# Gated recurrence and multiplicative feed-forward on one core: another layout for the first 512 tokens, ten operations for the decay rates, a last tile in two strips, and another order of the first fifteen chunks

## The chip, the core and the metric

The kernel runs on one core of a Trainium2 chip. A core has a matrix engine (TensorE, in the profile PE, its weight loads PEld), a vector engine (VectorE, DVE), a scalar engine (ScalarE, ACT), GpSimd (POOL) and SyncE (SP), which here issues the transfers. Each engine runs its own instructions strictly in the program's order and waits on semaphores for the others. The metric is the device time of one execution in microseconds; lower is better.

## The reference

The first half is a gated linear recurrence over 4 sequences of 5,824 tokens with 256 channels, the second a feed-forward block on the 23,296 tokens, with a product of two projections in its middle:

```python
# x, r_gate, i_gate: (4, 5824, 256); a_param: (256,)
a_base = 1.0 / (1.0 + np.exp(-a_param))
sig_r = 1.0 / (1.0 + np.exp(-r_gate));  sig_i = 1.0 / (1.0 + np.exp(-i_gate))
log_a = 8.0 * sig_r * np.log(np.clip(a_base, 1e-06, 1.0 - 1e-06))[None, None, :]
a_t = np.exp(log_a)
norm = np.sqrt(np.maximum(1.0 - a_t * a_t, 1e-06))
x_gated = norm * sig_i * x
for t in range(S):
    h = a_t[:, t] * h + x_gated[:, t]
    y[:, t] = h
# y as 23296 x 256; w1, w2: 256 x 1024; w3: 1024 x 1024; w_out: 1024 x 256
h = (y @ w1) * (y @ w2) @ w3
out = (h @ w_out).astype(np.float32)
```

## The kernel before

The 23,296 tokens are cut into 47 chunks, `sizes = [256, 256] + [512] * 44 + [256]`. Gates of chunks 0 and 1 are made together, as one of 512 tokens (`gates_of`, `width`, `part`). The kernel is a list of small steps, written out by hand as one string, `ORDER`; each word names a step and its chunk, and each engine gets its instructions in the order of the words. So a word further left on one engine can hold up everything behind it on that engine, and the transfers, all issued by SP, go in the order of their words too.

The words, for chunk c:

- `r i x`: loads of the three inputs (512 KB each); `Lw1. Lw2. Lw3. Lwo.` loads of weight pieces (512 KB each), `Cw1.` and so on their casts to bf16 on the engine that `W_ACT`, `W_DVE` or, failing both, GpSimd gives (L385, L387).
- `R I`: tanh of r and of i on ACT (L157, L159, L165). `p t`: plus one, times x (L170, L186, L189). `V U`: turning channels to partitions, on PE against the identity through PSUM (L197) or by a transposing transfer (L208), for r and for the gated x.
- `d`: the decay by an exponential (L220). `s`: its square (L228, L230; `DV_SQUARE` and `AC_SQUARE` give the engine). `q`: the root (L235). `g`: root times gated x on DVE (L245, L248). `h`: the scan on DVE (L266), one for each half of the channels. `y`: cast of the scan's result to bf16 (L278).
- `a c.m.q`: one up product with w1, two matmuls into one PSUM bank (L289, tile pa). `b c.m`: two up products with w2 (tile pb). `c c.m.q`: copy of pa to SBUF as bf16 (tile sa; L303 on DVE, L305 on ACT, by `DV_COPY`). `m c.m`: the product of sa and pb on DVE (L317, tile g_t).
- `D c.j`: the down product of 128 tokens, eight matmuls of 256 columns (L331, tile po) with a matrix folded from w3 and w_out. `e o`: its copy to SBUF and the store.
- `Ft Fc Fm Fe`: the folding itself, transpose of a piece of w3 (L392), copy, product with w_out (L403), copy (L438, L440).
- `A3. A0. A1. A2.`: the decay rates of the 256 channels from `a_param` (L412 to L434). `E`: the identity in bf16. `W`: two matmuls of the identity whose result nobody reads (L283, tile warm).

The tiles are rings of fixed size, among them `"r": 4, "i": 5, "x": 4`, and in PSUM `"po": 4` banks, which pa, po and all the turned tiles share, and `"pb": 2` of two banks each. A step that takes a slot waits for the reader of what was in it: with two pb slots, a `b` waits for the `m` two `b`s earlier; with four po slots, an `a` waits for the copy of the tile four earlier.

For chunks 0 and 1 every pa tile holds 256 columns of a bank of 512, and has its own copy of 128x256. In the last chunk (46) each `D` has its own PSUM tile, `e` alternates between DVE and ACT, and each 128 tokens are stored by one transfer.

Of the kernel before, what the change touches and what calls it, by code (L numbers as in the profile page):

```python
# [18 lines left out]
LOG1P = (2.00000001, 0.66666316, 0.40024854, 0.27961419, 0.28174657)  # L19
# [3 lines left out]
def kernel(  # L23
# [71 lines left out]
    DV_EVAC = {(2, 0), (8, 0), (8, 1), (9, 0), (9, 1)}
    FOLD_ACT = {('c', 7), ('e', 3), ('e', 4)}
    W_ACT = {('w1', 1), ('w2', 0), ('w3', 0)}
    W_DVE = set()
# [3 lines left out]
    WARM = [2] * 16  # L102
    RINGS = {"r": 4, "i": 5, "x": 4, "th_r": 3, "u": 2, "rt": 2, "ut": 6, "a": 6, "nrm": 6, "h": 2, "y": 4,
# [38 lines left out]
    def load(c, nm):  # L142
        n = width(c) // P
        t = ring(loads, [P, 4, D], F32, name=nm + "_t", tag=nm)
        nc.sync.dma_start(
            out=t[:, :n, :],
            in_=src[nm][starts[c]:starts[c] + width(c), :].rearrange("(p n) c -> p n c" if long_rows(c) else "(n p) c -> p n c", p=P))
        T[nm, c] = t
# [102 lines left out]
    def scan(c, cb):  # L251
        w = sizes[c]
        first = ("h", c) not in T
        if first:
            T["h", c] = ring(ypool, [P, NCB, CT], F32, name="h_t", tag="h")
        h = T["h", c][:, :, :w]
        a, n = (T[key, gates_of(c)][:, :, part(c)] for key in "an")
        if first:
            for b in range(1, B):
                if 0 < b * S - starts[c] < w:  # L260
                    nc.vector.memset(a[:, :, b * S - starts[c]:b * S - starts[c] + 1], 0.0)
        init = 0.0
        if starts[c] % S != 0:
            pw = sizes[c - 1]
            init = T["h", c - 1][:, cb, pw - 1:pw]
        nc.vector.tensor_tensor_scan(h[:, cb, :], a[:, cb, :], n[:, cb, :], init, ALU.mult, ALU.add)  # L266

    def cast(c, cb=None):
        w = sizes[c]
        if ("y", c) not in T:  # L270
            T["y", c] = ring(ypool, [P, NCB, CT], BF16, name="y_t", tag="y")
        key = c if cb is None else (c, cb)
        cbs = slice(None) if cb is None else cb
        y, h = T["y", c][:, cbs, :w], T["h", c][:, cbs, :w]
        if key in AC_CAST:
            nc.scalar.copy(out=y, in_=h)
        else:
            (nc.vector if key in DV_CAST else nc.gpsimd).tensor_copy(out=y, in_=h)  # L278

# [6 lines left out]
    def up(c, m, dst, w_sb):  # L286
        w = sizes[c]
        for cb in range(NCB):
            nc.tensor.matmul(out=dst[:, :w], lhsT=w_sb[:, cb, m * P:(m + 1) * P],  # L289
                             rhs=T["y", c][:, cb, :w], start=(cb == 0), stop=(cb == NCB - 1))  # L290

    def up_a(c, mp, q):
        T["pa", c, mp, q] = pp = ring(psum_o, [P, CT], F32, name="pa", tag="po")
        up(c, 2 * mp + q, pp, w1_sb)

    def up_b(c, mp):
        T["pb", c, mp] = pp = ring(psum_b, [P, 2, CT], F32, name="pb", tag="pb")
        for q in range(2):
            up(c, 2 * mp + q, pp[:, q, :], w2_sb)
# [7 lines left out]
    def copy(c, mp, q):  # L307
        w = sizes[c]
        if ("sa", c, mp) not in T:
            T["sa", c, mp] = ring(ffn, [P, 2, CT], BF16, name="sa", tag="sa")  # L310
        copy_to((c, mp, q) in DV_COPY, T["sa", c, mp][:, q, :w], T["pa", c, mp, q][:, :w])

    def product(c, mp):
        w = sizes[c]
        if ("g", c) not in T:
            T["g", c] = ring(ffn, [P, KD, CT], BF16, name="g_t", tag="g")
        nc.vector.tensor_mul(out=T["g", c][:, 2 * mp:2 * mp + 2, :w], in0=T["sa", c, mp][:, :, :w],  # L317
                             in1=T["pb", c, mp][:, :, :w])

    def pair(c, j2):  # L320
        return min(2, sizes[c] // P - 2 * j2)

    def down(c, j):
        if c == NCH - 1:
            T["po_last", j] = po = ring(psum_o, [P, D], F32, name="po", tag="po")
        else:
            if ("po", c, j // 2) not in T:
                T["po", c, j // 2] = ring(psum_o, [P, 2, D], F32, name="po", tag="po")
            po = T["po", c, j // 2][:, j % 2, :]
        for k in range(KD):  # L330
            nc.tensor.matmul(out=po,  # L331
                             lhsT=T["g", c][:, k, j * P:(j + 1) * P], rhs=wp_sb[:, k, :],
                             start=(k == 0), stop=(k == KD - 1), skip_group_check=True)
# [6 lines left out]
    def evac_last(c, j):  # L340
        if ("ot", c, j // 2) not in T:
            T["ot", c, j // 2] = ring(ffn, [P, 2, D], F32, name="ot", tag="ot")
        copy_to(j % 2 == 0, T["ot", c, j // 2][:, j % 2, :], T["po_last", j])

    def store_last(c, j):
        t0 = starts[c] + j * P
        nc.sync.dma_start(out=out[t0:t0 + P, :], in_=T["ot", c, j // 2][:, j % 2, :])
# [41 lines left out]
    def fold_t(mi):  # L389
        pt = ring(psum_o, [P, KD, P], BF16, name="ptw", tag="po")  # L390
# [25 lines left out]
    def rates_abs():  # L416
        nc.vector.tensor_copy(out=la4, in_=T["la"])
        nc.vector.scalar_tensor_tensor(out=zz, in0=la4, scalar=-1.0, in1=la4, op0=ALU.mult, op1=ALU.min)
# [5 lines left out]
    def rates():  # L424
        nc.vector.tensor_scalar(zd, zz, 2.0, None, op0=ALU.add)
        nc.vector.reciprocal(zd, zd)
        nc.vector.tensor_mul(out=zz, in0=zz, in1=zd)
# [14 lines left out]
    def last(c):  # L442
# [3 lines left out]
        "r": lambda c: load(c, "r"), "i": lambda c: load(c, "i"), "x": lambda c: load(c, "x"),  # L446
# [17 lines left out]
        r0 i0 x0 A3. E A0. A1. A2. R0.1 R0.0 W7 W10 V0.1 V0.0 W3 W14 W4 d0.1 s0.1 d0.0 s0.0 I0 q0.0 t0.0 t0.1 U0 g0  # L464
        h0.0 W1 W2 W12 W5 W13 W8 W0 W15 h0.1 q0.1 g1 h1.1 h1.0 Lw1.0 Cw1.0 y0.1 y0.0 i2 Lw2.0 I2 r2 Lw1.1 Cw2.0 a0.0.1
        a0.0.0 a0.1.0 a0.1.1 b0.0 R2 Cw1.1 x2 y1.1 y1.0 p2 t2.0 Lw3.2 Cw3.2 Lw2.1 Lwo.1 t2.1 c0.0.1 c0.1.1 c0.0.0
        c0.1.0 m0.0 V2 b0.1 a1.1.0 a1.1.1 b1.1 a1.0.1 d2.1 d2.0 s2.1 s2.0 q2 m0.1 c1.1.1 c1.1.0 m1.1 c1.0.1 a1.3.0
        b1.0 a1.0.0 a0.2.0 c0.2.0 c1.0.0 c1.3.0 Cw2.1 Ft2 W9 Fc2 a0.2.1 a1.3.1 U2 a1.2.0 m1.0 W11 b0.2 c0.2.1 c1.3.1
        c1.2.0 Cwo.1 Lwo.0 Cwo.0 g2 r3 r4 Lw3.1 i3 Lw3.0 Lw3.4 Lw3.5 x3 Lw3.3 Lw3.7 Lw3.6 i4 m0.2 h2.0 h2.1 R3 a0.3.1
        W6 a0.3.0 b0.3 c0.3.0 c0.3.1 a1.2.1 Fm2 b1.2 V3 R4 c1.2.1 V4 d3.0 d4.1 d3.1 d4.0 m0.3 y2 b1.3 Fe2 m1.2 m1.3  # L470
        a2.1.0 a2.0.1 b2.0 Cw3.1 a2.0.0 Ft1 I3 c2.0.0 c2.0.1 c2.1.0 Fc1 a2.2.0 b2.1 Fm1 m2.0 c2.2.0 Cw3.0 s4.0 p3
        Cw3.4 s3.1 s4.1 s3.0 q3 q4 Ft0 a2.1.1 Fe1 Fc0 c2.1.1 Cw3.5 t3.0 t3.1 Ft4 a2.3.1 Fc4 c2.3.1 Fm0 Ft5 Fm4 a2.2.1
        Fe4 c2.2.1 Cw3.7 Cw3.3 Cw3.6 Fe0 Fc5 m2.1 U3 g3 Fm5 a2.3.0 Ft7 b2.3 Ft3 c2.3.0 Fe5 h3.1 h3.0 r7 I4 Fc7 R7 Ft6
        b2.2 Fm7 V7 r5 R5 Fc3 Fm3 Fc6 Fe7 d7.1 Fe3 y3 a3.1.1 d7.0 s7.0 c3.1.1 x4 i5 r6 Fm6 i6 i8 I5 R6 V5 p4 t4.0 t4.1
        x5 r8 m2.3 Fe6 m2.2 b3.1 a3.1.0 a3.2.1 a3.2.0 c3.1.0 c3.2.1 I6 V6 U4 b3.2 a3.0.1 D0.1 D0.0 g4 h4.0 h4.1 c3.0.1
        c3.2.0 d5.1 I8 e0.0 d5.0 s7.1 a3.0.0 m3.1 c3.0.0 D1.1 a3.3.1 D1.0 a3.3.0 R8 c3.3.1 e1.0 d6.0 p5 y4 t5.0 t5.1
        s5.1 p6 m3.2 c3.3.0 r10 x6 r9 i7 o1.0 o0.0 r12 x8 V8 a4.1.0 b3.3 m3.3 b3.0 a4.1.1 c4.1.0 s5.0 d6.1 s6.0 s6.1
        a4.2.0 b4.1 a4.0.1 a4.0.0 m3.0 c4.1.1 c4.0.1 c4.0.0 q7 q5 D3.0 D3.1 q6 c4.2.0 m4.1 a4.3.1 U5 g5 h5.0 h5.1
        c4.3.1 e3.0 R9 I7 b4.0 D2.3 D2.1 a4.2.1 D2.0 D2.2 c4.2.1 e2.1 m4.0 e2.0 b4.2 p8 t6.1 t6.0 y5 R10 t8.0 p7 t8.1
        a4.3.0 U6 a5.0.0 a5.1.0 b4.3 d8.1 c4.3.0 c5.0.0 d8.0 R12 s8.0 i10 m4.2 g6 h6.1 h6.0 x7 o3.0 r11 y6 D3.3 a5.0.1  # L480
        a5.1.1 c5.0.1 D3.2 c5.1.0 e3.1 I10 b5.1 m4.3 a5.2.1 a5.2.0 b5.0 V9 c5.1.1 m5.1 i9 V10 o2.0 o2.1 r16 i11 c5.2.1
        d9.1 I9 c5.2.0 d9.0 d10.0 R11 U8 i13 r13 x9 x10 V11 r15 m5.0 a6.0.1 a6.0.0 c6.0.1 c6.0.0 a6.1.1 b5.2 m5.2
# [151 lines left out]
```

## Time and profile before

| what | us |
|---|---|
| time, median of 3 runs (511.63 to 512.12) | 511.82 |
| the profiled execution's own time | 511.82 |
| its span in the profile | 510.0 |
| PE, ACT, DVE, POOL busy in the span | 502.2, 463.3, 429.8, 318.2 |
| first matmul of an up product starts | 13.30 |
| last matmul ends, about | 506.8 |

The span runs from the first instruction to the last; 1.8 us of the execution lie around it. Busy time is the union of an engine's instructions. In the views by time the first number is the start and the second a duration, both in microseconds; in the groups the numbers after the bar are the sum in microseconds and the mean of one in nanoseconds, and what stands in brackets or after the last bar is idle time before an instruction and who ended it.

### The profile page before, as it was taken

Reading aid. Unit: us, or ns where it says so; the run is one execution under the profiler, and the core shown is the slowest. Engines: PE = TensorE matmul, PEld = TensorE weight load, DVE = VectorE, ACT = ScalarE, POOL = GpSimd, SP = SyncE. Lnnn points to the kernel's source line nnn. Section 1 sums busy time; section 2 is a strip of 40 time slices with the busy share of each in tenths; the row PEclk is TensorE's granted clock in tenths of the full one; section 3 lists DMA queues with packets and bytes.
Section 4 is the critical chain, followed back from the end, with each engine's and each line's share of the span. In section 5 each row is a group of like instructions: output and inputs, shape, how many; then the busy total and the mean of one; then the engine's idle time right before and its main releaser. Section 6 shows DMA issues by size and latency. Waiting matters only on the chain.

```text
span 510.0 us, 8879 instructions
## 1 busy us (share of the span) xinstructions
PE 502.2 (98%) x3217; PEld 308.2 (60%) x3217; DVE 429.8 (84%) x417; ACT 463.3 (91%) x711; POOL 318.2 (62%) x274
## 2 busy tenths in 40 slices
PE   7999999999999999999999999999999999999997
PEld 3777655665565656556666556565566655656566
DVE  5999999999999789878879799878877797959762
ACT  7999999998999999999999999998998979888543
POOL 3775878557558936965786973956647568580200
PEclk9999999999999999999999999999999999999999
DMA  8999999999989997896999996898786895252313
GB/s 319 407 413 307 379 275 276 304 302 257 309 232 282 303 282 248 191 322 184 256 306 317 262 285 163 233 245 227 206 250 151 231 319 149 91 164 64 66 48 105
DMA packets 177904, 124.06 MB, mean 243 GB/s; under 512 B 87362, under 2 KB 173892, under 8 KB 177860
## 3 DMA queue, kind: packets, MB, share of 16 engines
q1 hardware_dynamic: 177856, 123.50, 85.2%
q8 instruction: 25, 0.41, 0.3%
q14 instruction: 19, 0.16, 0.1%
q10 hardware_dynamic: 4, 0.00, 0.0%
HBM read 78.91 MB, written 23.86 MB: 201 GB/s over the span
## 4 chain that ended last, share of the span: by engine, by line
PE 90%; ACT 4%; DVE 2%; issue 2%; DMA 1%; DVEq 0%; ACTq 0%
PE po L331 30%; PE pb L289 29%; PE pa L289 28%; PE pw L403 1%; ACT sa L305 1%; PE ptr L197 1%; DVE g_t L317 1%; DMA r_t<-in_r_gate_dram 1%; PE ptw L392 1%; DVE sa L303 1%; DVE h_t L266 1%; ACT L165 1%; ACT L235 1%; ACT nrm L235 0%; ACT i_t L165 0%
## 5 line engine op out<-in xcount | busy, mean ns | idle before, releaser
L317 DVE TENSOR_TENSOR g_t<-sa,pb 128x1024 bf16<-128x1024 bf16 (+1 forms) x188 | 218.6, 1180 | 60.6 <-PE pb L289 29.0
L289 PEld LDWEIGHTS <-w_sb 128*128 128x128 bf16 x1504 | 146.5, 98 | 144.0 <-issue 3.4
L305 ACT CAST sa<-pa 128x512 bf16<-128x512 f32 (+1 forms) x336 | 180.9, 588 | 27.7 <-PE pa L289 17.6
L289 PE MATMUL pa<-y_t,w_sb 128*128 128x512 bf16 (+1 forms) x752 | 190.6, 372 | 0.4 <-ACT sa L305 0.2
L289 PE MATMUL pb<-y_t,w_sb 128*128 128x512 bf16 (+1 forms) x752 | 185.2, 372 | 0.6 <-DVE g_t L317 0.6
L331 PE MATMUL po<-wp_sb,g_t 128*128 128x256 bf16 x1456 | 178.0, 273 | 0.0
L331 PEld LDWEIGHTS <-g_t 128*128 128x128 bf16 x1456 | 142.4, 98 | 40.6 <-issue 0.5
L278 POOL CAST y_t<-h_t 128x1024 bf16<-128x1024 f32 (+2 forms) x49 | 52.5, 1074 | 146.0 <-DVE h_t L266 142.2
L189 POOL TENSOR_TENSOR u_t<-i_t,x_t 128x512 bf16<-128x512 f32 (+1 forms) x90 | 122.2, 1374 | 4.1 <-issue 2.0
L266 DVE TENSOR_TENSOR_SCAN h_t<-a_t,h_t,nrm 128x512 f32<-128x512 f32 (+1 forms) x92 | 120.8, 1343 | 1.6
L230 POOL TENSOR_TENSOR nrm<-a_t 128x512 f32<-128x512 f32 x74 | 83.0, 1139 | 12.9 <-ACT a_t L220 10.1
L220 ACT ACTIVATE a_t<-rt,la 128x512 f32<-128x512 bf16 (+1 forms) x82 | 66.0, 823 | 0.0
L305 ACT COPY ot<-po 128x512 f32<-128x512 f32 x86 | 50.5, 591 | 12.0 <-PE po L331 11.8
L248 DVE SCALAR_TENSOR_TENSOR nrm<-nrm,ut 128x1024 f32<-128x1024 f32 (+1 forms) x39 | 53.3, 1368 | 5.8 <-ACT nrm L235 5.8
L170 POOL TENSOR_SCALAR i_t<-i_t 128x1024 f32<-128x1024 f32 (+1 forms) x44 | 52.9, 1204 | 7.9 <-ACT i_t L165 7.9
L165 ACT ACTIVATE i_t<-i_t 128x1024 f32<-128x1024 f32 (+1 forms) x46 | 48.9, 1064 | 0.1
L235 ACT ACTIVATE nrm<-nrm 128x1024 f32<-128x1024 f32 (+1 forms) x47 | 48.3, 1041 | 0.2
L159 ACT ACTIVATE th_r<-r_t 128x1024 bf16<-128x1024 f32 (+1 forms) x41 | 43.5, 1060 | 0.0
L303 DVE CAST sa<-pa 128x512 bf16<-128x512 f32 (+1 forms) x40 | 23.4, 615 | 0.6 <-PE pa L289 0.5
L235 ACT ACT_TABLE_LOAD x17 | 21.8, 1283 | 0.3
L165 ACT ACT_TABLE_LOAD x9 | 11.5, 1283 | 0.2
L283 PE MATMUL warm<-ident 128*128 128x512 bf16 x32 | 10.1, 457 | 0.0
(55 smaller groups left out, 119.3 us busy)
## 6 DMA issues: line engine op xcount, KB each, us to landing
r_t<-in_r_gate_dram SPq DMA_DIRECT2D x45, 512.0 KB, 5.3
i_t<-in_i_gate_dram SPq DMA_DIRECT2D x45, 512.0 KB, 5.6
x_t<-in_x_dram SPq DMA_DIRECT2D x45, 512.0 KB, 5.5
out_dram<-ot SPq DMA_DIRECT2D x90, 256.0 KB, 3.3
wf<-in_moe_w_dram SPq DMA_DIRECT2D x12, 512.0 KB, 10.5
wf<-in_moe_w_out_dram SPq DMA_DIRECT2D x2, 512.0 KB, 10.6
rt<-th_r SPq DMA_TRANSPOSE x41, 4.4
ut<-u_t SPq DMA_TRANSPOSE x39, 4.1
```

Source lines behind the costliest of these rows:

```text
L165: nc.scalar.activation(out=t[:, :n, :], in_=t[:, :n, :], func=AF.Tanh, scale=0.5)
L170: (nc.vector if c in DV_PLUS else nc.gpsimd).tensor_scalar(t, t, 1.0, 1.0, op0=ALU.add, op1=ALU.mult)
L189: (nc.vector if (c, half) in DV_HALF else nc.gpsimd).tensor_mul(out=u, in0=t, in1=xt)
L220: nc.scalar.activation(out=a, in_=pr, func=AF.Exp, scale=la4[:, cb:cb + 1], bias=la4[:, cb:cb + 1])
L230: (nc.vector if (c, cb) in DV_SQUARE else nc.gpsimd).tensor_mul(out=n, in0=a, in1=a)
L235: nc.scalar.activation(out=n, in_=n, func=AF.Sqrt, scale=-1.0, bias=1.0)
L248: nc.vector.scalar_tensor_tensor(out=n, in0=n, scalar=1e-3, in1=T["pu", c][:, :, cols], op0=ALU.max, op1=ALU.mult)
L266: nc.vector.tensor_tensor_scan(h[:, cb, :], a[:, cb, :], n[:, cb, :], init, ALU.mult, ALU.add)
L289: nc.tensor.matmul(out=dst[:, :w], lhsT=w_sb[:, cb, m * P:(m + 1) * P], rhs=T["y", c][:, cb, :w], start=(cb == 0), stop=(cb == NCB - 1))
L305: nc.scalar.copy(out=dst, in_=src_ps)
L317: nc.vector.tensor_mul(out=T["g", c][:, 2 * mp:2 * mp + 2, :w], in0=T["sa", c, mp][:, :, :w], in1=T["pb", c, mp][:, :, :w])
L331: nc.tensor.matmul(out=po, lhsT=T["g", c][:, k, j * P:(j + 1) * P], rhs=wp_sb[:, k, :], start=(k == 0), stop=(k == KD - 1), skip_group_che ...
```

## The change

- Chunks 0 and 1 share one h, one y and one g tile of 512 tokens. Their up products stay in halves of 256 tokens (`HALVED = 4` means all four pairs), but the two products q = 0 and 1 of a pair go into one PSUM bank and are copied together: 8 copies of 128x512 where there were 16 of 128x256. The down products of these 512 tokens are `D0.0` to `D0.3`, with two copies and two stores of 256 tokens.
- r of chunk 0 is one load (the `load` function gets an argument for half the columns, which no word uses).
- The rates: with z = exp(|x|), one over z + 0.5 takes the place of z / (z + 2), and the powers of two go into the constants: ten DVE operations in `A2.` where there were eleven.
- The last 128 tokens are two strips of 128 output columns: sixteen matmuls of 128 columns in two PSUM tiles, two copies (DVE, then ACT), two stores of 64 KB.
- `ORDER` is new from the start to chunk 14's scan; the 1,678 words behind that are the same. Which engine does which square, copy and cast is new up to chunk 15. The number of `W` words stays 16.

```diff
-LOG1P = (2.00000001, 0.66666316, 0.40024854, 0.27961419, 0.28174657)
+LOG1P = tuple(c / 2 ** (2 * k + 1) for k, c in
+              enumerate((2.00000001, 0.66666316, 0.40024854, 0.27961419, 0.28174657)))
...
-    DV_PLUS = {16}
+    DV_PLUS = set()
-    DV_SQUARE = {(0, 1), (11, 0)}
+    DV_SQUARE = {(0, 0), (0, 1), (5, 1), (9, 0)}
-    DV_CAST = set()
-    AC_CAST = set()
+    DV_CAST = {(1, 1)}
+    AC_CAST = {(1, 0)}
...
-    DV_EVAC = {(2, 0), (8, 0), (8, 1), (9, 0), (9, 1)}
-    FOLD_ACT = {('c', 7), ('e', 3), ('e', 4)}
-    W_ACT = {('w1', 1), ('w2', 0), ('w3', 0)}
-    W_DVE = set()
+    DV_EVAC = {(0, 0), (0, 1), (4, 1), (5, 1), (6, 1), (9, 0), (9, 1)}
+    FOLD_ACT = {('e', 0), ('e', 4), ('e', 5), ('e', 7)}
+    W_ACT = {('w2', 0), ('w3', 3)}
+    W_DVE = {('w1', 1)}
+    HALVED = 4
...
+    def in_half(c, mp):
+        return c < 2 and mp < HALVED
+
+    def span(c, mp):
+        return part(c) if in_half(c, mp) else slice(0, width(c))
...
     def up_a(c, mp, q):
+        if in_half(c, mp):
+            if ("pa", c, mp) not in T:
+                T["pa", c, mp] = ring(psum_o, [P, 2, sizes[c]], F32, name="pa", tag="po")
+            up(c, mp, q, T["pa", c, mp][:, q, :], w1_sb)
+            return
...
+        if in_half(c, mp):
+            copy_to((c, mp, q) in DV_COPY, T["sa", c, mp][:, :, :sizes[c]], T["pa", c, mp])
+            return
...
+    def strips(c, j):
+        whole = not (c == NCH - 1 and j == sizes[c] // P - 1)
+        return [slice(0, D)] if whole else [slice(0, P), slice(P, D)]
...
     def rates():
-        nc.vector.tensor_scalar(zd, zz, 2.0, None, op0=ALU.add)
-        nc.vector.reciprocal(zd, zd)
-        nc.vector.tensor_mul(out=zz, in0=zz, in1=zd)
+        nc.vector.tensor_scalar(zd, zz, 1e30, 0.5, op0=ALU.min, op1=ALU.add)
+        nc.vector.reciprocal(zz, zd)
...
     ORDER = """
-        r0 i0 x0 A3. E A0. A1. A2. R0.1 R0.0 W7 W10 V0.1 V0.0 W3 W14 W4 d0.1 s0.1 d0.0 s0.0 I0 q0.0 t0.0 t0.1 U0 g0
-        h0.0 W1 W2 W12 W5 W13 W8 W0 W15 h0.1 q0.1 g1 h1.1 h1.0 Lw1.0 Cw1.0 y0.1 y0.0 i2 Lw2.0 I2 r2 Lw1.1 Cw2.0 a0.0.1
-        a0.0.0 a0.1.0 a0.1.1 b0.0 R2 Cw1.1 x2 y1.1 y1.0 p2 t2.0 Lw3.2 Cw3.2 Lw2.1 Lwo.1 t2.1 c0.0.1 c0.1.1 c0.0.0
-        c0.1.0 m0.0 V2 b0.1 a1.1.0 a1.1.1 b1.1 a1.0.1 d2.1 d2.0 s2.1 s2.0 q2 m0.1 c1.1.1 c1.1.0 m1.1 c1.0.1 a1.3.0
-        b1.0 a1.0.0 a0.2.0 c0.2.0 c1.0.0 c1.3.0 Cw2.1 Ft2 W9 Fc2 a0.2.1 a1.3.1 U2 a1.2.0 m1.0 W11 b0.2 c0.2.1 c1.3.1
+        r0 i0 x0 Lw1.1 Lw1.0 r2 i2 Lw2.0 Lw3.2 x2 E W13 A3. A0. A1. A2. R0.1 R0.0 W3 W10 V0.0 V0.1 I0 t0.1 d0.0 s0.0
+        d0.1 s0.1 q0.0 t0.0 Cw1.1 q0.1 Cw1.0 R2 I2 W5 W8 W0 U0 W4 W11 W6 W12 W7 W9 W2 g0 h0.1 h0.0 y0.1 y0.0 a0.0.1
+        a0.1.1 a0.1.0 a0.0.0 V2 W15 Cw2.0 g1 h1.1 h1.0 y1.1 y1.0 d2.1 Lw2.1 Lwo.1 Lwo.0 r3 Cw3.2 d2.0 s2.1 s2.0 q2
+        b0.0 c0.0.0 c0.1.0 a1.1.0 m0.0 Ft2 a1.1.1 c1.1.0 b0.1 a1.0.0 a0.2.1 a1.0.1 b1.1 m0.1 Fc2 b1.0 a0.2.0 p2 t2.0
+        t2.1 U2 c1.0.0 m1.1 Cw2.1 m1.0 a0.3.1 W14 b0.2 a1.3.1 W1 a1.3.0 c0.2.0 g2 Cwo.1 Cwo.0 r4 Lw3.0 Lw3.5 i3 Lw3.1
...
```

## The prediction

> **What bounds the kernel now.** I read the page's busy times first, then busy time by stretches, then the timeline of the start, the groups with shapes kept apart, the chain of waits near 120 us, and the timeline of the end.
>
> ```profile
> PE 502.2 (98%) x3217; PEld 308.2 (60%) x3217; DVE 429.8 (84%) x417; ACT 463.3 (91%) x711; POOL 318.2 (62%) x274
> ...
> PE 90%; ACT 4%; DVE 2%; issue 2%; DMA 1%; DVEq 0%; ACTq 0%
> ...
> 0.00:13.30 13.30, 9.94 (x44) 4.14 (x45) 7.66 (x25) 10.15 (x13) 4.04 (x10) 1.00 0.86 322
> 13.30:30.00 16.70, 16.26 (x142) 11.69 (x141) 16.01 (x30) 16.64 (x25) 11.44 (x12) 1.00 1.04 411
> 30.00:155.00 125.00, 124.39 (x849) 78.69 (x847) 121.45 (x130) 122.09 (x176) 83.99 (x73) 1.00 1.06 302
> ```
>
> PE ends 90% of the chain. In the stretches the numbers after the length are PE, PEld, DVE, ACT and POOL busy, then clock, DMA share and GB/s. From 30 to 155 us PE idles 0.6 us of 125, but DVE (121.45) and ACT (122.09) are nearly as full. Before 30 us the transfers run at 411 GB/s without a pause. PE has a fixed amount of work, so four places can change: the time to the first useful matmul, holes in PE until about 155 us, the steps behind it (same words), and the tail.
>
> ```profile
> 4.40 1.15 ACT L157 ACTIVATE th_r<-r_t 128x512 bf16<-128x512 f32 x2 [1.33 <-DMA r_t<-in_r_gate_dram]
> 6.00 2.77 PE L283 MATMUL warm<-ident 128*128 128x512 bf16 x6
> 8.79 1.55 POOL L387 CAST w_sb<-wf 128x1024 bf16<-128x1024 f32 x1 [0.50 <-DMA wf<-in_moe_w_dram]
> 9.43 1.15 ACT L235 ACTIVATE nrm<-nrm 128x512 f32<-128x512 f32 x2
> 9.84 3.62 PE L283 MATMUL warm<-ident 128*128 128x512 bf16 x16
> 13.30 1.04 PE L289 MATMUL pa<-y_t,w_sb 128*128 128x256 bf16 x8
> ```
>
> The first load is there at 4.4 us, the fourth at 8.8: 1.3 to 1.5 us a load (512 KB at some 400 GB/s is 1.3). Warm matmuls keep PE until 13.30.
>
> **The change part by part.**
>
> *First useful matmul.* ACT now does tanh of i (1.06) ahead of the decays: after r's tanh (5.55) and the second load (about 5.7) to 6.75; decays to 8.1; table load 1.28; roots from 9.4. Before they began at 9.43, with tanh of i between decays and load: no change. DVE takes both squares of the first chunks (one from POOL) and a weight cast; g x starts when x is in (about 6.9): two of 0.69, two squares of 0.69, to 9.45. That feeds U0, and 14 warm matmuls stand behind U0 where 16 did: 14 x 0.216 = 3.02, so about 13.0 instead of 13.30. The rates lose one operation of about 0.2, but two warm matmuls (2 x 0.43) now stand before their transpose; they end near 5.5 instead of 5.25, under the 6.75 at which the decays can start. **-0.3** (-0.6 to +0.2; nothing else can be saved here, as y is ready only at about 12.6).
>
> *The clock, a rule that speaks against it.* Warm matmuls are 0.43 apart at 6 us and 0.216 from 9.84 (3.62 for 16, 2.77 for 6). The Trainium skill, "TensorE: Matmul & The Clock Gate", section "Part 1: The HAM clock gate", says that full rate is granted only after about 3.4 us of sustained activity, in a window that runs freely. The six warm matmuls before U0 end near 8.8 here too and U0 waits until 9.45, a hole of 0.65 where 0.3 was. By the strict rule the 14 could run slowly: 6.0 instead of 3.0, +3. The trace tolerated 0.8 at 4.3 us, so I take zero and keep the rule for the upper end.
>
> *13 to 27 us.* Loads move on SP. w1's second half, w1's first half, r2 and i2 now stand ahead of w2's first piece, so that is the eighth load and not the sixth: at 1.36 each about 13.9, not 11.2. Its cast (ACT, 1.03) stands behind tanh of r2 and i2 and ends near 15.0; `b0.0`, at 14.17 before, starts near 15.05. The four `a`, V2 and a warm pair cover until 14.75; hole 0.3. The next transpose, Ft2, wants w3's third piece: ninth load, about 15.4, POOL cast 1.04, so 16.5, while PE is free at 15.7; hole 0.8. On POOL that cast now precedes p2 (1.05) and two t2 (1.28 each), which end near 20.0 (19.27 before); U2 waits for them: hole 0.55. Behind them stand the casts of w2's second half and w_out, to 22.95, just when Fm2 wants them (23.2). Three warm pairs (1.3) stay in this stretch in both. Before, the holes and warm pairs took 2.0 of 13.30 to 26.17; now about 2.95, and chunk 2's first up product starts near 26.6 instead of 26.17 with the same work done. That is 0.43 later, and as the start was 0.3 earlier, the stretch itself costs **+0.73** (-0.3 to +2.0; the loads' times are inferred and POOL's queue is tight).
>
> ```profile
> L305 ACT CAST sa<-pa 128x512 bf16<-128x512 f32 x322 | 176.3, 597 | 22.4 <-PE pa L289 13.7 <-DVE g_t L317 7.5
> L305 ACT CAST sa<-pa 128x256 bf16<-128x256 f32 x14 | 4.7, 375 | 5.2 <-PE pa L289 4.0 <-DVE g_t L317 1.3
> L303 DVE CAST sa<-pa 128x512 bf16<-128x512 f32 x30 | 19.8, 681 | 0.6 <-PE pa L289 0.5
> L303 DVE CAST sa<-pa 128x256 bf16<-128x256 f32 x10 | 3.7, 416 | 0.0
> L230 DVE TENSOR_TENSOR nrm<-a_t 128x512 f32<-128x512 f32 x2 | 1.4, 690 | 1.3 <-ACT a_t L220 1.3
> ```
>
> *The load of DVE and ACT.* Neighbours on DVE overlap by 0.08 and on ACT by 0.1, so a step costs its mean less that. DVE, by the word lists up to chunk 14: first-chunk copies ten of 0.336 become four of 0.60 (-0.96); squares +2 (+1.22); one `p` less (0.927 in its row, -0.85); later copies +2 (+1.2); evacuations +2 (+1.2); fold copies +1 (+0.6), fold scalings -2 (-0.68); rates -0.2; new, a weight cast f32 to bf16 of 1024 columns and a y cast of 256. Those two have no row on DVE: nearest are the 0.93 of `p` with the same elements (upper) and half of it (lower); I take 0.7 and 0.2. Sum **+2.4 on DVE**; likewise about **-1.6 on ACT** (weight cast -0.95, fold copy -0.9, copies and evacuations -1.65, squares +1.06, scalings +0.54, y +0.27), less on POOL (four squares). It costs time only where PE waits for DVE. DVE idled about 4.0 us between 13 and 151 us, so 2.1 of the 2.4 (the part after chunk 2's g) can lie there if the order fits. I followed the new words by hand with the durations above, waiting for each ring's reader: PE waits nowhere over 0.15 us from 27 to 147, while the old order loses about 1.1 after 27 us. The largest of that is here:
>
> ```profile
> 119.48 2.11 issue
> 121.59 1.20 DVE g_t L317
> 122.83 1.02 PE pb L289 x4
> ...
> 119.34 2.33 DVE L266 TENSOR_TENSOR_SCAN h_t<-a_t,h_t,nrm 128x512 f32<-128x512 f32 x1
> 117.23 3.36 POOL L189 TENSOR_TENSOR u_t<-i_t,x_t 128x512 bf16<-128x512 f32 x2
> ```
>
> A scan took 2.33 instead of 1.28 (the last two lines, from DVE's and POOL's timelines), beside a stretched POOL product, and PE then waited 0.6 at 122.8. The Trainium skill, "SBUF — State Buffer", section "Who interferes with whom", says that a DVE instruction with two SBUF inputs and a GpSimd instruction that reads SBUF exclude each other, the later one waiting. By it each of the two added squares could cost up to a POOL product (1.3), +2.6. The trace shows it rarely: the median of 88 scans is 1.28, with POOL busy 62%. I expect zero or one such event, in either order. A hand-followed order has fewer waits than a real one, so of the 1.1 I credit 0.4: **-0.4** (-1.1 to +1.5, the upper end if DVE's extra work doesn't fit). Behind 155 us the words are equal and PE is full: zero, only shifted.
>
> *Tail.*
>
> ```profile
> 505.98 0.42 DVE L303 COPY ot<-po 128x256 f32<-128x256 f32 x1 [1.69 <-PE po L331]
> 506.43 1.21 SPq L347 DMA_DIRECT2D out_dram<-ot  x2
> 506.90 0.37 ACT L305 COPY ot<-po 128x256 f32<-128x256 f32 x1 [1.21 <-PE po L331]
> ```
>
> Sixteen matmuls of 128 columns for eight of 256: turned tiles show 0.056 each, 0.90 against 0.87. The last copy shrinks from 0.37 to about 0.26 (two sizes on ACT, 0.60 and 0.37, give 0.11 per 128 columns), its store halves. The first strip's copy and store lie beside the second's matmuls. One more SP issue (0.35) is done before. **-0.2** (-0.4 to +0.1).
>
> Sum: -0.3 + 0.73 - 0.4 - 0.2 = -0.17, on the profiled execution's 511.82, which is also the median: about 511.6. The single load of r changes nothing: r0 was one load of 512 tokens already, so that item does not do what its name says against this kernel.
>
> **The rivals.** Under 0.2%, 1.0 us, counts as no change, about what a measurement can tell.
>
> 1. *It cancels* (0.41): early loss against later gain and tail, 511.6 (510.7 to 512.7).
> 2. *The stream is as dense as followed by hand, and the start slips less* (0.27): -1.1 instead of -0.4, holes at Ft2 and U2 half as large (-0.7): 510.3. For it: those holes hang on two transfers and one POOL queue; against: it needs every wait to be met.
> 3. *DVE becomes the bound before 155 us* (0.18). Place: `b13.0`, which before followed `m12.1` within 0.2 us. Chunk 2's g ends about 1.0 later, the rest of DVE's list is 2.1 longer; if its idle time stays 4.0, PE comes there 3.1 late: 514.7; with half given back, 512.7. It decides where DVE's idle time shrinks by less than 1.9. Against: ACT gets room, and it was the other full engine.
> 4. *POOL's chain slips* (0.14): the ninth load one transfer later, 1.3, passes through cast, p2, t2, U2 and Fm2: 513.0. It decides where the cast of w3's third piece starts 1.2 later than 15.4.
>
> **How the numbers follow.** Of rival 1, 0.31 is within 1.0 us and 0.05 on either side; of 2, 0.24 faster and 0.03 within; of 3, 0.15 slower and 0.03 within; of 4, 0.10 and 0.04. Sum: faster 0.29, same 0.41, slower 0.30. The range 509.9 to 513.9 leaves out the ends of 2 and 3 and the cold clock, under 0.2 together.
>
> **What would show it.** First up product near 13.0; Ft2 near 16.5 and U2 near 20.0; chunk 2's first `a` near 26.6; `b13.0` within 1 us of 153.4; last copy 0.26. Wrong if the clock is still half in the 14 warm matmuls, if PE has over 1.5 us of holes between 30 and 155 us, or if chunk 2 starts before 25.5.

## The result, and the profile after

The changed kernel takes 511.31 us (median of 20 executions, 510.87 to 512.05), the kernel before, beside it on the same chip, 512.01 (511.58 to 514.76). The ratio is 0.9984, with a 95% interval of 0.9977 to 0.9991: 0.7 us less by the medians, 0.8 by the ratio. That is clear of noise, and still under the 0.2% taken here as no change. The profiled execution has a span of 509.1 where the one of before had 510.0.

The starts of a few words in the two traces show where the 0.9 us of the spans come from:

| place in the words | before, us | after, us | difference |
|---|---|---|---|
| first up product of chunk 0, `a0.0.1` | 13.30 | 13.11 | -0.19 |
| first up product of chunk 2 | 26.16 | 26.38 | +0.21 |
| `b13.0` | 153.44 | 152.63 | -0.81 |
| last down product, `D46.1` | 505.78 | 504.91 | -0.87 |
| last store landed | 509.01 | 508.12 | -0.89 |

So the first up product comes 0.19 earlier, the stretch from there to chunk 2 loses 0.40, the stretch from 26 to 153 us gains 1.02, and the tail gains nothing. The page of the changed kernel, its busy times and the engines' shares of the chain:

```profile
PE 501.7 (99%) x3225; PEld 308.3 (61%) x3225; DVE 431.8 (85%) x417; ACT 461.5 (91%) x708; POOL 318.0 (62%) x269
...
PE 92%; ACT 3%; DMA 2%; POOL 1%; DVE 1%; issue 1%; SPq 1%; ACTq 0%; DVEq 0%
```

Its busy time by stretches (length, then PE, PEld, DVE, ACT, POOL, granted clock, DMA share, GB/s):

```profile
0.00:13.30 13.30, 10.31 (x45) 4.34 (x46) 8.33 (x26) 10.26 (x13) 2.79 (x9) 1.00 0.85 322
13.30:30.00 16.70, 15.61 (x138) 11.22 (x137) 15.79 (x25) 16.42 (x23) 12.22 (x12) 1.00 1.04 412
30.00:155.00 125.00, 125.00 (x857) 79.18 (x855) 122.83 (x134) 121.46 (x176) 85.14 (x70) 1.00 1.05 303
```

From 30 to 155 us PE is busy for all of 125.00 us, where it was for 124.39; DVE went from 121.45 to 122.83 and now idles 2.17. From 13.3 to 30 PE is busy 0.65 less than before.

Busy time hides part of a hole, because the end of a matmul is modelled: in these traces 256 columns are drawn 0.27 long and start 0.109 apart. So holes are counted here from start to start, with 0.056, 0.109 and 0.216 for 128, 256 and 512 columns without a wait. The matmuls in each of the two stretches are the same before and after. From `a0.0.1` to chunk 2's first up product the holes are 1.48 before and 1.88 after, which is the 0.40; from there to `b13.0` they are 1.43 before and 0.40 after, which is the 1.02. Of the 1.43, one hole at 122.8 us is 0.74; two more, at 28.98 and 136.9, are 0.21 and 0.20. After, the longest is 0.14.

The groups with shapes kept apart, the lines that answer to those of before (sum and mean after the bar):

```profile
L322 ACT CAST sa<-pa 128x512 bf16<-128x512 f32 x324 | 177.1, 596 | 21.9 <-PE pa L299 14.9 <-DVE g_t L337 6.0
L322 ACT CAST sa<-pa 128x256 bf16<-128x256 f32 x8 | 2.8, 380 | 5.2 <-PE pa L299 4.0 <-DVE g_t L337 1.3
L320 DVE CAST sa<-pa 128x512 bf16<-128x512 f32 x36 | 23.5, 684 | 1.4 <-PE pa L299 0.8
```

The small copies on DVE are gone, and ACT's fell from 14 to 8; a merged copy costs what any 128x512 copy costs.

The timeline of the start (start, duration, in brackets the idle time before the instruction and what ended it):

```profile
6.32 2.77 PE L287 MATMUL warm<-ident 128*128 128x512 bf16 x6
9.63 0.62 PE L200 MATMUL ptr<-ident,u_t 128*128 128x128 bf16 x8 [0.54 <-DVE u_t L189]
10.09 3.19 PE L287 MATMUL warm<-ident 128*128 128x512 bf16 x14
13.11 1.04 PE L299 MATMUL pa<-y_t,w_sb 128*128 128x256 bf16 x8
...
16.47 0.62 PE L425 MATMUL ptw<-ident,w_t 128*128 128x128 bf16 x8 [0.43 <-POOL w_t L416]
...
20.07 0.51 PE L200 MATMUL ptr<-ident,u_t 128*128 128x128 bf16 x6 [0.46 <-POOL u_t L192]
...
17.35 0.69 DVE L320 CAST sa<-pa 128x512 bf16<-128x512 f32 x1 [0.79 <-PE pa L299]
...
20.94 1.28 DVE L248 SCALAR_TENSOR_TENSOR nrm<-nrm,ptr 128x512 f32<-128x512 f32 x2
22.73 2.49 DVE L270 TENSOR_TENSOR_SCAN h_t<-a_t,h_t,nrm 128x512 f32<-128x512 f32 x2
25.28 1.04 POOL L282 CAST y_t<-h_t 128x1024 bf16<-128x1024 f32 x1 [2.32 <-DVE h_t L270]
```

The first four lines: U0 waits 0.54 and its eight transposes still take 0.62, so the clock is full there. The next two are the holes at Ft2 and U2. Behind Ft2 stands `a1.1.1`, and its copy on DVE (17.35) has waited 0.79; from there on DVE has no idle time until y2's scans are done. The last three lines are the end of that chain: g2, the two scans, and y2 on POOL, which ends at 26.33, 0.05 ahead of chunk 2's first up product at 26.38. PE waits for this list twice here, 0.18 ahead of `b1.3` (for m0.3 behind the scans) and 0.09 for y2. The same chain before, from its timeline:

```profile
20.75 1.28 DVE L245 SCALAR_TENSOR_TENSOR nrm<-nrm,ptr 128x512 f32<-128x512 f32 x2
...
25.07 1.04 POOL L278 CAST y_t<-h_t 128x1024 bf16<-128x1024 f32 x1 [2.85 <-DVE h_t L266]
```

There y2 ended at 26.11 and the product began at 26.16, and PE had waited 0.02 for it: before, PE and DVE arrive together. Chunk 2 starts 0.21 later because y2 ends 0.21 later, and that is g2's 0.19 in DVE's list.

At the place of the largest hole of before, the timelines of DVE and POOL after:

```profile
120.20 1.28 DVE L270 TENSOR_TENSOR_SCAN h_t<-a_t,h_t,nrm 128x512 f32<-128x512 f32 x1
...
120.30 2.01 POOL L233 TENSOR_TENSOR nrm<-a_t 128x512 f32<-128x512 f32 x1
```

Before, the scan was there second, beside a running POOL product, and took 2.33. Now the scan is first and takes 1.28; the POOL square behind it takes 2.01 (mean of its form 1.15), and no engine's wait of that stretch is put down to it.

### The profile page after: what moved, and what is told of

Its sections match the earlier page's. It is cut to its first block, busy times and chain, and to the rows that moved or that the text cites. A ratio compares the mean times of both kernels' runs of the same rounds, so it can differ in the third digit from the quotient of the medians.

```text
span 509.1 us, 8891 instructions
## 1 busy us (share of the span) xinstructions
PE 501.7 (99%) x3225; PEld 308.3 (61%) x3225; DVE 431.8 (85%) x417; ACT 461.5 (91%) x708; POOL 318.0 (62%) x269
## 4 chain that ended last, share of the span: by engine, by line
PE 92%; ACT 3%; DMA 2%; POOL 1%; DVE 1%; issue 1%; SPq 1%; ACTq 0%; DVEq 0%
PE po L357 30%; PE pb L299 29%; PE pa L299 29%; DMA wf<-in_moe_w_dram 2%; PE pw L436 1%; ACT sa L322 1%; PE ptr L200 1%; PE ptw L425 1%; POOL u_t L192 0%; DVE h_t L270 0%; SPq L151 0%; ACT ot L322 0%; SPq L407 0%; ACT L168 0%; ACT L238 0%
## 5 line engine op out<-in xcount | busy, mean ns | idle before, releaser
L357 PE MATMUL po<-wp_sb,g_t 128*128 128x256 bf16 (+1 forms) x1464 | 177.6, 272 | 0.0
L282 POOL CAST y_t<-h_t 128x1024 bf16<-128x1024 f32 (+2 forms) x47 | 53.8, 1145 | 140.2 <-DVE h_t L270 136.1
L233 POOL TENSOR_TENSOR nrm<-a_t 128x512 f32<-128x512 f32 x70 | 78.4, 1137 | 7.0 <-ACT a_t L223 4.0
L322 ACT COPY ot<-po 128x512 f32<-128x512 f32 x84 | 49.1, 589 | 13.2 <-PE po L357 12.9
L173 POOL TENSOR_SCALAR i_t<-i_t 128x1024 f32<-128x1024 f32 (+1 forms) x45 | 55.4, 1233 | 8.3 <-ACT i_t L168 8.3
L320 DVE CAST sa<-pa 128x512 bf16<-128x512 f32 x36 | 23.5, 684 | 1.4 <-PE pa L299 0.8
L231 ACT ACTIVATE nrm<-a_t 128x512 f32<-128x512 f32 x18 | 11.4, 645 | 0.0
```

Of the source, the lines that this page charges most:

```text
L173: (nc.vector if c in DV_PLUS else nc.gpsimd).tensor_scalar(t, t, 1.0, 1.0, op0=ALU.add, op1=ALU.mult)
L233: (nc.vector if (c, cb) in DV_SQUARE else nc.gpsimd).tensor_mul(out=n, in0=a, in1=a)
L322: nc.scalar.copy(out=dst, in_=src_ps)
L357: nc.tensor.matmul(out=po, lhsT=T["g", c][:, k, j * P:(j + 1) * P], rhs=wp_sb[:, k, cols], start=(k == 0), stop=(k == KD - 1), skip_group_ ...
```

## The experiments

Ratios are to the kernel before, with their 95% intervals. As single traces differ in their first loads by some tenths, starts are also given as distances from `a0.0.1`.

**1. The changed start, the old rest.**

```diff
-        r4 Lw3.0 Lw3.5 i3 Lw3.1 Lw3.4 x3 Lw3.3 Lw3.6 Lw3.7 r7
+        r4 Lw3.1 i3 Lw3.0 Lw3.4 Lw3.5 x3 Lw3.3 Lw3.7 Lw3.6 i4
...
-        a2.0.0 a2.0.1 b2.0 a2.1.0 c2.0.1
+        a2.1.0 a2.0.1 b2.0 Cw3.1 a2.0.0
...
```

(Against the changed kernel. The words of before go on to the end, with `D1.0 D1.1 e1.0 o1.0` called `D0.2 D0.3 e0.1 o0.1`, and with its engines for squares, copies and casts from chunk 2 on; the weight loads from `r4` on are in the old order too.)

> The changed kernel's words up to chunk 2's first up product, then the words and engine choices of the kernel before from there to the end (its tail in two strips is kept). Theory A, the parts add up: chunk 2's first up product near 26.4, later than before by about 0.2, and then the order of before loses its 1.0 us again between 27 and 155 (a hole of about 0.6 at b9.3 behind m9.2), so about 0.2 above before, 512.2. Theory B, the gain sits in the start (fewer copies, shared tiles leave DVE and ACT freer for what follows): the later holes shrink, and the time is 511.5 or less.

Measured: 512.68 us, ratio 1.0012 (1.0003 to 1.0021). Chunk 2 starts at 26.38, as in the changed kernel. The hole of before is back, in the timeline of PE:

```profile
122.80 1.02 PE L295 MATMUL pb<-y_t,w_sb 128*128 128x512 bf16 x4 [0.58 <-DVE g_t L333]
```

`b13.0` starts at 153.41, where before has 153.44. So the gain belongs to the order and the choice of engines behind 26 us, and theory B falls. But the 0.21 lost in the start costs nothing here: with the old order `a2.2.0` waits until 28.98 anyway (a hole of 0.21 in before, none in this run), and from there to 190 us PE's instructions in the two traces start within 0.04 of each other. The old order had slack where the new one has none. The median is 0.6 above before's, while the profiled execution, the fastest of its eleven (511.83), is level with it; where the slower ones lost it is not shown, as this is the only trace of the run.

**2. The old start, the changed rest.** The words and engines of before up to chunk 2; each pair of up products keeps one copy, at the place of the later of its two words (the cut is against before).

```diff
-        c0.0.1 c0.1.1 c0.0.0 c0.1.0
+        c0.0.0 c0.1.0
...
-        c0.2.0 c1.0.0 c1.3.0 Cw2.1 Ft2 W9 Fc2 a0.2.1 a1.3.1 U2 a1.2.0 m1.0 W11 b0.2 c0.2.1 c1.3.1 c1.2.0
+        c1.0.0 Cw2.1 Ft2 W9 Fc2 a0.2.1 a1.3.1 U2 a1.2.0 m1.0 W11 b0.2 c0.2.0 c1.3.0
...
```

> The words of before up to chunk 2's first up product (each pair of up products still copied once, from one bank), then the changed kernel's words and engine choices. Theory A, the parts add up: first up product near 13.3, chunk 2's near 26.2, no hole over 0.15 from 27 to 155, b13.0 near 152.4: about 1.0 under before, 511.0, and 0.2 under the changed kernel. Theory B, the later order only fits behind its own start: POOL's and ACT's queues differ there, holes of 0.5 to 1 us come back, 511.5 to 512.0.

Measured: 511.83 us, ratio 1.0000 (0.9991 to 1.0009): the time of theory B, but not for its reason. The start itself got worse. From PE's timeline:

```profile
21.46 0.38 PE L295 MATMUL pa<-y_t,w_sb 128*128 128x256 bf16 x2 [1.25 <-ACT sa L318]
```

`a1.2.0` waits 1.25 for a merged copy that now stands on ACT behind q2's table load and root (19.40 to 20.46), so chunk 2 starts only at 27.04. Behind it the changed order keeps what it gains: from chunk 2's start to `b13.0` it takes 126.44 us, against 126.25 in the changed kernel and 127.27 before. From 37 us to the end every PE instruction lies 0.84 to 0.86 behind its place in the changed kernel, without drift, and to 153 us every DVE instruction too: that order gives nothing back and catches nothing up. And merging two copies was no gain in this place, where the one copy waits for both products.

**3. One word on POOL.**

```diff
-        Cw3.2 d2.0
+        p2 Cw3.2 d2.0
...
-        a0.2.0 p2 t2.0
+        a0.2.0 t2.0
```

> The changed kernel with one word moved: chunk 2's plus one ahead of the cast of w3's third piece on POOL. It can run from 13.95 to 15.0, while POOL idles, so both products and U2 end 0.6 to 0.9 earlier, and the hole of 0.62 at U2 goes. Theory A, chunk 2's first up product waits for y2, whose chain runs on DVE from the copy behind Ft2 through g2 and the two scans: it stays within 0.15 of 26.38 and the time at 511.3. Theory B, the holes of PE add up, as in my prediction's sum: chunk 2 starts 0.5 to 0.6 earlier and the time is 510.7.

Measured: 511.36 us, ratio 0.9987 (0.9979 to 0.9996), the changed kernel's. U2 no longer waits (19.58), yet chunk 2 starts 13.42 behind `a0.0.1` (13.27 in the changed kernel). Theory A holds: the holes of PE in the start don't add up to chunk 2's start, y2's chain sets it. The hole moved to the warm pair behind `a0.3.1` (0.48). The 0.15 between 13.42 and 13.27 means nothing: run 4, with the same words here as the changed kernel, has 13.66. What stays the same is the distance from Ft2 to chunk 2's first up product: 9.90 in the changed kernel, 9.89, 9.90 and 9.91 in runs 1, 4 and 7, and 9.88 in this run, without the hole at U2. So a delay of Ft2, which hangs on the load and cast of w3's third piece, passes through DVE's list to chunk 2 in full, and the hole at U2 costs nothing. The move also had a price, in the timelines of POOL and DVE:

```profile
14.00 1.49 POOL L173 TENSOR_SCALAR i_t<-i_t 128x1024 f32<-128x1024 f32 x1 [0.88 <-ACT i_t L168]
...
14.57 1.07 DVE L282 CAST y_t<-h_t 128x256 bf16<-128x256 f32 x1
```

Plus one takes 1.49 instead of 1.05 beside the scans, and the cast y1.1 on DVE 1.07 instead of 0.27. In the changed kernel POOL idles there.

**4. The last 128 tokens whole.**

```diff
-        whole = not (c == NCH - 1 and j == sizes[c] // P - 1)
+        whole = True
```

> The changed kernel with its last 128 tokens whole, as before: eight matmuls of 256 columns, one copy of 0.37, one store of 128 KB. Theory A: the strips gave nothing, as their second store stands behind the first on SP (0.92 for the two issues against about 0.35 for one): 511.3, and from D46.1's first matmul to the last landing 3.2 as in both kernels. Theory B, my prediction's term of 0.2: 511.5, with 3.4 for that stretch.

Measured: 511.53 us, ratio 0.9993 (0.9984 to 1.0001); against the changed kernel's interval this leaves open anything from nothing to several tenths, so the trace decides. From `D46.1`'s start to the last landing it takes 3.23, as before (3.23); with strips 3.21. The strips are worth 0.02. The timeline of the changed kernel's end shows the parts:

```profile
505.11 0.74 DVE L320 COPY ot<-po 128x256 f32<-128x256 f32 x2 [1.69 <-PE po L357]
505.56 1.35 SPq L376 DMA_DIRECT2D out_dram<-ot  x3
506.05 0.27 ACT L322 COPY ot<-po 128x128 f32<-128x128 f32 x1 [1.23 <-PE po L357]
```

The last copy ends 0.09 sooner behind `D46.1`'s start (1.40 against 1.49) and the half store lands 0.17 sooner behind its issue (1.20 against 1.37); but SP's two issues take from 506.00 to 506.92 and end 2.01 behind `D46.1`'s start, where the single one ended at 1.86.

**5. The chain to y2 shortened.**

```diff
-        Cw3.2 d2.0 s2.1 s2.0 q2 b0.0 c0.0.0 c0.1.0 a1.1.0 m0.0 Ft2 a1.1.1 c1.1.0 b0.1 a1.0.0
+        p2 Cw3.2 d2.0 s2.1 s2.0 q2 b0.0 c0.0.0 c0.1.0 a1.1.0 m0.0 a1.1.1 c1.1.0 b0.1 Ft2 a1.0.0
...
-        h2.0 h2.1
+        h2.0 y2.0 h2.1 y2.1
...
-        b1.3 y2 Fe2
+        b1.3 Fe2
```

> The changed kernel with three moves in the start: plus one of chunk 2 ahead of the cast of w3's third piece on POOL; Ft2 behind b0.1, so that the product a1.1.1 and its copy on DVE don't stand behind that cast; y2 cast in two halves, the first while the second scan runs. Theory A, chunk 2 waits for the chain on DVE and POOL that ends with y2: DVE's list runs 0.7 earlier and y2 ends another 0.5 earlier, so PE becomes the bound, chunk 2's first up product starts near 25.5, and as the changed order has no hole behind it, the time is 0.7 to 0.9 lower, 510.5. Theory B, the loads of w3's pieces, which land at 26 to 34, hold the folds: holes come back between 27 and 36, 511.2.

Measured: 511.15 us, ratio 0.9984 (0.9971 to 0.9997). Theory A was wrong: chunk 2 starts 13.47 behind `a0.0.1`, where the changed kernel has 13.27 and run 4 13.66. Two engines shared what they can't share. Plus one, moved to 14.06, made the two scans of the second 256 tokens take 2.13 instead of 1.39. That put y1.1 behind the cast of w3's piece on POOL, and it took 1.06 instead of 0.27. From the timelines of DVE and POOL:

```profile
15.70 1.06 DVE L282 CAST y_t<-h_t 128x256 bf16<-128x256 f32 x1
...
15.53 1.08 POOL L416 CAST w_t<-wf 128x1024 bf16<-128x1024 f32 x1 [0.29 <-DMA wf<-in_moe_w_dram]
```

(In run 6 y1.1 starts at 15.50, 0.02 ahead of that cast, and takes 0.26.) Together that is 1.53, about twice the 0.79 that moving Ft2 had won. And half of y2 beside the second scan brought little, as the next run shows in the same way. Theory B has nothing for it either; no hole of PE over 0.22 stands between 27 and 37, and one matmul missing from the trace looks like 0.22. The profiled execution took 511.94, 0.8 more than the median; its first up product is 0.79 later than in the changed kernel.

**6. The same, two warm pairs less, and chunk 2 ahead of `b1.3`.**

```diff
-        a0.3.1 W14 b0.2 a1.3.1 W1 a1.3.0
+        a0.3.1 b0.2 a1.3.1 a1.3.0
...
-        m0.3 b1.3 Fe2 m1.2 m1.3 a2.0.0 a2.0.1 b2.0
+        Fe2 m0.3 m1.2 a2.0.0 a2.0.1 b1.3 m1.3 b2.0
```

> As the kernel before it in this list, and the two warm pairs ahead of and behind b0.2 (W14, W1) are taken out, chunk 2's first two up products stand ahead of b1.3, and one fold scaling and two products on DVE follow that order. Theory A: PE reaches chunk 2 about 0.9 earlier still where its inputs allow, near 24.9, and the time is 510.0 to 510.3. Theory B, inputs bind: y2 ends near 25.1 and w_out's cast near 22.2, so only 0.3 of the 0.9 comes, or the w3 loads hold the folds: 510.5 to 511.2.

Measured: 511.52 us, ratio 0.9989 (0.9980 to 0.9998). Chunk 2 now does start 12.43 behind `a0.0.1`, 0.84 earlier than in the changed kernel; and from 37 to 153 us DVE's instructions lie 0.55 to 0.58 behind the changed kernel's, where `a0.0.1` is 0.52 behind. All of the 0.84 is gone. The timelines of DVE and POOL say where:

```profile
24.05 1.25 DVE L270 TENSOR_TENSOR_SCAN h_t<-a_t,h_t,nrm 128x512 f32<-128x512 f32 x1
...
24.19 2.08 POOL L282 CAST y_t<-h_t 128x512 bf16<-128x512 f32 x2 [1.88 <-DVE h_t L270]
...
27.61 0.69 DVE L337 TENSOR_TENSOR g_t<-sa,pb 128x512 bf16<-128x512 bf16 x1 [0.80 <-PE pb L299]
```

The half cast starts 0.14 behind the scan and ends 0.42 after it (25.72): two halves take 2.08, the whole cast took 1.04. And m1.3 waits 0.80 for `b1.3`, which I had put behind chunk 2's products. PE was early, DVE lost its lead in that wait, and what DVE loses is not made up.

**7. Four copies from ACT to DVE.**

```diff
-    DV_COPY = {...}
+    DV_COPY = {..., (4, 0, 0), (6, 2, 0), (8, 2, 1), (10, 1, 1)}
```

> The changed kernel with four copies of 128x512 of chunks 4, 6, 8 and 10 on DVE instead of ACT: 2.4 us more on DVE, where it idles 2.17 between 30 and 155. Theory A, the prediction's rival of DVE as the bound was near: b13.0 comes 0.5 to 2.4 later, 511.8 to 513.5. Theory B, DVE still has room and ACT's relief helps: holes on PE under 0.3 in that stretch, 511.3 to 511.6.

Measured: 515.21 us, ratio 1.0059 (1.0046 to 1.0073). Theory A, and beyond its numbers. Against the changed kernel DVE's instructions are 0.18 late up to 63 us (the start of this execution), 2.19 late at `c6.1.1`, 3.17 at `c8.0.1`, 4.09 at `h12.0`, and stay so. Four copies of 0.68 (0.60 with the overlap of neighbours) cost 3.9 us, nearly 1.0 each. Who waited for whom from 30 to 155 us (sum, times, longest):

```profile
PE pb L296 <- DVE g_t L334: 0.9, 2, 0.7
PE pa L296 <- DVE sa L317: 0.8, 1, 0.8
PE pa L296 <- DVE ot L317: 0.5, 1, 0.5
PE pa L296 <- POOL y_t L279: 0.4, 1, 0.4
```

The changed kernel has no such line in that stretch. So with 2.17 of idle time DVE is at the bound as well as PE, and idle time that is left over does not sit where more work would need it. The trace shows where the 3.9 come from. The copies' own length is 2.4. Three other DVE instructions of the stretch now start just behind one on POOL and are longer than in the changed kernel: a scan 1.87 instead of 1.46 (at 70.02), a scan 1.78 instead of 1.28 (77.81), a product of root and gated x 2.04 instead of 1.25 (135.16), together 1.7. The first of them, with the POOL instruction it met, from the timelines of DVE and POOL:

```profile
70.02 1.87 DVE L267 TENSOR_TENSOR_SCAN h_t<-a_t,h_t,nrm 128x512 f32<-128x512 f32 x1
...
69.76 1.06 POOL L170 TENSOR_SCALAR i_t<-i_t 128x1024 f32<-128x1024 f32 x1
```

From 63 us to h12.0 DVE is 3.75 us longer busy (its other instructions are some 0.3 shorter) and 0.16 longer idle: one of the new copies waited 0.53 for its own matmuls (at 101.06), other waits are shorter.

**8. No warm matmuls behind U0.**

```diff
-        U0 W4 W11 W6 W12 W7 W9 W2 g0
+        U0 g0
```

> The changed kernel without the 14 warm matmuls behind U0; PE idles from U0's end near 10.1 until the first y, about 13.05. Theory A, the clock rule of my prediction: after such a pause the first matmuls run at half rate, 0.43 instead of 0.216 for 512 columns, for some 3 us: Ft2 and what follows come late, chunk 2's first up product 0.5 to 1.5 later, 511.8 to 512.8. Theory B, the rate stays full after a pause of 3 us: everything at its place, 511.3.

Measured: 513.26 us, ratio 1.0020 (1.0010 to 1.0030), some 1.9 above the changed kernel; theory A, and beyond its numbers: chunk 2's first up product starts 15.08 behind `a0.0.1` instead of 13.27, 1.8 later and not 0.5 to 1.5. Busy time and clock by stretch in this run:

```profile
13.30:20.00 6.70, 6.61 (x41) 4.98 (x41) 4.22 (x8) 6.01 (x9) 3.92 (x5) 0.56 1.05 401
```

and PE's timeline:

```profile
13.39 1.86 PE L299 MATMUL pa<-y_t,w_sb 128*128 128x256 bf16 x8 [3.17 <-POOL y_t L282]
```

After a pause of 3.17 the granted clock is 0.56 up to 20 us; 256 columns take 0.213 instead of 0.109 from 13.6 to 19.2. The 14 matmuls whose result nobody reads are worth about 1.9 us by the medians; single executions of this run took 511.77 to 514.10.

No run beat the changed kernel by more than the spread. Left untried: more warm matmuls ahead of V0 and U0, and Ft2 behind `b0.1` alone. The shorter rates and the merged copies were not run by themselves, nor was any part of the new order between 27 and 155 us.

## Why the prediction came out right, point by point

The time was right, 511.6 forecast and 511.31 measured, and some of that is luck. The sum had a change of -0.17; the traces have -0.89. The four terms were off by +0.11, -0.33, -0.62 and +0.18, and 0.06 came behind `b13.0`. "No change" held because the gain stayed under 0.2%; it did not cancel, as rival 1 had it.

- *First useful matmul, -0.3:* -0.19. U0 came at 9.63, not 9.45; the 14 warm matmuls and the first y (ready at 13.05, not 12.6 as I had written) ended almost together.
- *The clock, taken as zero:* right for the profiled execution, where the hole before U0 (0.54) cost nothing. But the reason given was wrong. The hole of 0.8 at 4.3 us that "the trace tolerated" lay where the clock was still half (V0's eight transposes behind it took 1.13, the warm matmuls 0.43 each, and the trace's clock record is full only from 9.16), so it had nothing to lose. And the clock is not settled once for the kernel. The words up to 13 us are the same in runs 5 and 6, and there U0 took 1.04 and `a0.0.1` began at 13.90 and 13.62:

```profile
9.78 1.04 PE L200 MATMUL ptr<-ident,u_t 128*128 128x128 bf16 x8 [0.45 <-DVE u_t L189]
```

(from the timeline of run 5). The rule has its cost, 0.42 in these executions by U0's durations alone, and run 8 shows what stands behind it.

- *13 to 27 us, +0.73:* +0.40. The events were right: `b0.0` at 15.22 (15.05 forecast), Ft2 at 16.47 (16.5), U2 at 20.07 (20.0), holes of 0.36, 0.59 and 0.62 (0.3, 0.8, 0.55). The step that failed is the next one, in which I added the holes and warm pairs up to chunk 2's start. Chunk 2 hangs on Ft2 through DVE's list to y2, and run 3 showed it: take the hole at U2 away, and chunk 2 does not move. It was late by what g2 was late, 0.2. The sum had two slips besides. From 2.0 to 2.95 is 0.95, not 0.73. And before, holes and warm pairs take 2.77 of the stretch (1.48 and 1.29), not 2.0, because most of these holes are short and hidden by modelled ends; after, they take 3.17.
- *The load of DVE, +2.4, and of ACT, -1.6:* busy times changed by +2.0 and -1.8; the two estimates, 0.7 and 0.2 for the casts, measured 0.69 and 0.27.
- *27 to 155 us, -0.4:* -1.02. This is the mis-sized term. Following the words by hand gave -1.1, and I credited a third of it because a hand-followed order has fewer waits than a real one. It had no more waits: the only holes over 0.1 are of 0.13 and 0.14. Runs 1 and 2 put the gain in this order and its engines; which words of it make the gain, no run separates.
- *The port shared by DVE and POOL, zero or one event:* zero events that cost, in the changed kernel; the one of before is gone, and it alone was 0.74 of PE's holes.
- *Tail, -0.2:* -0.02. I had written that one more SP issue is done before. It is not: the second issue ends 0.15 later behind `D46.1` than the single one did, and run 4 gives the same 3.23 without strips.
- *Rival 2* (dense as followed by hand, start slips less) is what came nearest in mechanism behind 27 us; its 510.3 was too low because the stretch before slipped by 0.40, where it has 0.03, and the tail gave nothing. *Rival 3* (DVE becomes the bound) did not happen at `b13.0`, but its mechanism is one step away: run 7. My point of decision, DVE's idle time shrinking by less than 1.9, was wrong; it shrank by 1.4 between 30 and 155 us and cost nothing. *Rival 4* (POOL's chain slips): the cast of w3's third piece began at 15.38, not 1.2 later than 15.4.

## What to carry to other kernels

Holes of an engine add up to a delay only if nothing else ends later: before you sum them, find the instruction that the next stage waits for in both kernels, here y2, and follow it back to the wait that sets it, here Ft2. Count holes from start to start, not from busy time. In this kernel, whose order had no hole left, a later start passed through to the end unchanged (run 2), and work added to DVE, nearly as full as PE, cost more than its own length (run 7), because it moved other DVE instructions behind running POOL instructions. Cutting the last transfer in two paid nothing here, as the second issue stood behind the first.

## What the runs showed of the hardware

- DVE and POOL hold each other up one whole instruction at a time, and the one that comes second waits. Second scan 2.33 instead of 1.28 behind a POOL product (before, run 1); POOL's square 2.01 instead of 1.15 behind a scan (after); POOL's first half of y2 1.52 behind a scan where the second half took 0.61 (run 6); a DVE cast of 256 columns 1.07 instead of 0.27 beside POOL's plus one (run 3). In these traces the second one ends 0.1 to 0.2 less than its own length behind the first one's end: a scan of 1.28 ends 1.08 behind it (before) and 1.07 twice (run 7), the half of y2 0.41, the cast 0.14. The Trainium skill, "SBUF — State Buffer", section "Who interferes with whom", says that whoever issues first gets the shared pair of ports for the whole instruction, and that casts too can take it; the runs agree. I had weighed it by the median of the scans, which hides it: what counts is who comes second at the places where PE waits.
- The moment at which PE's clock becomes full differs between executions with the same words before it. By the traces' clock records it is 4.93 in run 4, 8.9 to 9.6 in the changed kernel and in runs 1, 3, 7 and 8, 11.15 and 10.81 in runs 5 and 6. Once full it outlasted a pause of 2.06 in run 4 and fell in one of 3.17 in run 8. From run 4's timeline:

```profile
9.47 0.62 PE L200 MATMUL ptr<-ident,u_t 128*128 128x128 bf16 x8 [2.06 <-DVE u_t L189]
```

In run 8 the clock is full from 8.97, half from 12.38 to 19.21 and then full; the half stretch is 6.83, twice 3.41, and the full stretches up to the end of the other traces' records, 498.35, 501.76 and 505.17, differ by 3.41 too. So the clock changes in steps of 3.41, at a phase that differs between executions. Busy time by such steps in run 8 (the clock column shows 1.00 where no record stands yet, so the first line's clock was not full):

```profile
5.56:8.97 3.41, 3.38 (x14) 1.59 (x14) 2.35 (x7) 3.23 (x4) 0.00 (x0) 1.00 0.97 346
8.97:12.38 3.41, 0.79 (x9) 0.55 (x9) 3.19 (x6) 3.37 (x5) 1.15 (x2) 1.00 1.04 417
12.38:15.79 3.41, 2.40 (x15) 1.88 (x15) 3.13 (x7) 2.70 (x4) 0.95 (x2) 0.50 1.03 411
15.79:19.21 3.42, 3.42 (x21) 2.40 (x20) 1.47 (x3) 3.33 (x6) 3.10 (x3) 0.50 1.06 391
```

PE was busy 3.38 in the step that ended in a full clock, 0.79 in the one that ended in half, 2.40 in the one that left it half, 3.42 in the next, which gave it back. The other traces fit. In the changed kernel the step to 5.90 had 2.58 of PE and left the clock half, the one to 9.31 had 3.19 and made it full; in run 5 the steps to 7.74 and 11.15 had 2.36 and 2.96; in run 4 two steps of 1.92 and 2.29 kept a full clock. Over the ten traces the least that made it full is 2.87 (run 6), the most that did not is 2.69 (run 5). So what a pause costs depends on how it lies to the steps. The Trainium skill, "TensorE: Matmul & The Clock Gate", section "Part 1: The HAM clock gate", tells of a window that runs freely; a pause that is harmless in one execution and costs 0.4 us in another is what one would see then, and these records agree.
